# Order of the parts of y, quarter-array score products and the first weight signs in a fused gated-recurrence and SwiGLU kernel

## The chip, the cores and the metric

The kernel runs on one core of a Trainium2 chip. A core has five engines that work side by side: TensorE (PE) for matrix products, VectorE (DVE) and ScalarE (ACT) for elementwise work, GpSimd (POOL), and SyncE (SP), which only issues DMAs here. Products go to PSUM[...]; other operands lie in SBUF. The metric is the time of the whole program on the device, in microseconds, lower is better. A profile is one execution recorded instruction by instruction.

## The reference

Two stages in 32-bit floats. First a gated linear recurrence over 4 batches, 8 heads, 768 steps and head size 48:

```python
f = 1.0 / (1.0 + np.exp(-f_logit))
for t in range(S):
    state = f[:, :, t, :, None] * state + np.einsum('bhd,bhe->bhde', k[:, :, t], v[:, :, t])
    y[:, :, t] = np.einsum('bhd,bhde->bhe', q[:, :, t], state)
```

Its output is laid out as 3072 tokens of 384 numbers, and then a feed-forward block is computed with weights of 384x1536, 384x1536 and 1536x384:

```python
g = x @ w_gate
silu = g * (1.0 / (1.0 + np.exp(-g)))
val = x @ w_val
return silu * val @ w_out
```

The weights arrive as 64-bit floats and are turned into 32-bit ones on the chip.

## The kernel before, in words

**Tiling.** A unit is one chunk of 128 steps of one batch: six chunks c by four batches b, 24 units, in the order of chunks. Within a unit, two heads share the 128 partitions: one in rows 0 to 47, one in rows 64 to 111 (`par` is 0 or 1), and there are four such pairs (`a`). Running products of the gates scale k and q (`kT`, `qT`), so that a chunk needs no loop over steps. The function `attention(u)` is a generator with 15 steps per unit:

- *Scores* (L695 to L700): for each head, kT times qT, a 128x128 square, into two banks, one for each `par`. The contraction runs over 48 rows, so two heads can be in the array at once.
- *Mask* (L719): DVE multiplies the two banks with the causal triangle into `A`.
- *State decay* (L599): `decayed` is the state of the chunk before, times the chunk's whole decay.
- *y* (L734 to L759): for b = 0, 1, 2 and c > 0, y is built transposed in two banks from two parts. The state's part is `decayed` times `qT` (L742), with 48 rows and 64 columns, so it uses quadrants of the array. The masked part is v times `A` (L746), with 128 rows and 64 columns. ACT copies both banks to `yT` (L750), and ten small DMAs carry the heads to their rows of `xT[c]` (L757), through SP in chunk 1 and through POOL afterwards. For b = 3, and for chunk 0, another form is used (L767) that ACT copies straight into xT; its state part uses a block-diagonal copy of the state, `diagonal`.
- *dS* (L785 to L789): k transposed times v, the chunk's addition to the state, in column halves of the array. The last chunk has none. Then DVE (ACT in chunk 0) adds it to the state (L794, L797).

**Feed-forward.** Chunk 0 is computed plainly (`mlp_plain`, L836 and L859), beside the conversion of the weights. Chunks 1 to 5 use a scheme with 15 products in place of 18 for the hidden layer (L1052) and 7 in place of 8 for the output (L1151, L1214), with sums of weights and tokens made by DVE.

**Weights.** `weight_piece` makes a piece of 32-bit weights from 64-bit ones in two steps. `sizes` runs on ACT: a copy of the low words (L491), for pieces in the list `SIGNED` also a Sign operation on the top 16 bits (L494), and an absolute value (L495). `join` runs on DVE: a clamp (L505), a shift (L508, or L512 with a second operation), for pieces that are not in `SIGNED` a masking of the top 16 bits (L514), and an addition (L502, L510 or L516). The first two pieces are split in two parts each, of 128x384; the others have 128x768.

**Order.** PE, DVE, ACT and SP have a fixed order (`in_order`): steps of `attention` and of the weights are placed among the feed-forward products by written due times (`EARLY`, `JOINS_AT`, `SCORES`, `CHAINS`; `in_turn_of_time`). In chunks 2 to 5 the y of unit b, its dS and the scores of unit b+1 come due at the same moment (`times`: y at o, dS at o + 0.01, scores at s + 0.02, where o of one unit is s of the next), so on PE they stand one behind the other. In chunk 1 they are apart. Banks for scores come from a shared pool of attention banks, or from the pools of the feed-forward products (`score_bank`); from chunk 2 on the attention pool has three banks, used in turn.

Of the kernel before, what the change touches and what calls it, by code (L numbers as in the profile page):

```python
# [9 lines left out]
FP32 = mybir.dt.float32  # L10
# [280 lines left out]
def short_path(ctx, tc, ident, least, judge, q, k, v, f_logit, moe_w_gate, moe_w_val, moe_w_out, out):  # L291
# [9 lines left out]
    nc = tc.nc  # L301
    B, H, S, D = q.shape
    C = 128
    NCH = S // C
    HP = H // 2
    W = 64
# [9 lines left out]
    SQUARES = 2  # L316
# [3 lines left out]
    att = ctx.enter_context(tc.tile_pool(name="att", bufs=1))  # L320
# [30 lines left out]
    start = const.tile([128, HP * N1], FP32, tag="start", name="start")  # L351
# [27 lines left out]
    decayed = const.tile([128, HP, W], FP32, tag="decayed", name="decayed")  # L379
# [53 lines left out]
    def load(u, what="fkqv"):  # L433
        b, c = units[u]
        rows = slice(c * C, (c + 1) * C)
        inputs = dict(f=f_logit, k=k, q=q, v=v)
        for nm in "fqkv" if c >= SQUARES else "fvkq" if by_squares(u) else "fkqv":
            src = inputs[nm]
            if nm not in what:
                continue  # L440
            if nm == "v":
                dst = v_of(u)
            elif not by_squares(u):
                dst = raw[nm][u % NRAW]
            else:
                since = len(traced)
                for n in range(4):
                    at = Q * (1 - n % 2)
                    (nc.sync if c >= SQUARES else nc.gpsimd).dma_start(
                        out=rooms[nm][Q * n:Q * (n + 1), at:at + HP * RUN].rearrange("t (a e) -> t a e", a=HP),  # L450
                        in_=src[b, n // 2::2, rows, :].rearrange("a (t i) d -> t a (i d)", i=NI))
                if c < SQUARES:
                    by_pool.extend(ins for ins in traced[since:] if ins.engine == mybir.EngineType.Pool)
                    keep_order(by_pool[-5:])
                continue
            queue = nc.gpsimd if nm == "v" and c < SQUARES and (by_squares(u) or u in (1, 2)) else nc.sync
            queue.dma_start(out=dst[:, :, 0:D], in_=src[b, :, rows, :].rearrange("h t d -> t h d"))
# [71 lines left out]
    NW = 2  # L529
    FIRST = 2  # L530
    NPART = 2
    SIGNED = (4, 6, 7, 8, 9, 11, 15, 16, 17)

    def add_piece(dst, src, parts=1):
        fetch, *rest = weight_piece(dst, src, parts, len(fetches) in SIGNED)
        fetches.append(fetch)
        for group, fs in zip((sizes, joins), rest):
            group += fs
# [13 lines left out]
    xT = {}  # L552

    def rows_of(par):
        return slice(W * par, W * par + D)
# [3 lines left out]
    def bank(name):  # L559
        return banks[-1].tile([128, 512], FP32, tag="a", name=name)  # L560
# [15 lines left out]
    def attention(u):  # L576
        b, c = units[u]
# [58 lines left out]
        kT = att.tile([128, HP, C], FP32, tag="kT", name="kT")  # L636
        qT = att.tile([128, HP, C], FP32, tag="qT", name="qT", bufs=2)
# [8 lines left out]
        n = HP * N1  # L646
# [17 lines left out]
        if turned:  # L664
# [5 lines left out]
            for r in range(NI):  # L670
                turn_queue.dma_start(out=turn[:, :, :, r, :].rearrange("t i a e -> t (i a) e"),
                                  in_=beside[Q * r:Q * (r + 1)].rearrange("t i (a e) -> t (i a) e", e=Q))
# [23 lines left out]
        sc = [score_bank(u) for _ in range(2)]  # L696
        for a in range(HP):
            for par in range(2):
                r = rows_of(par)
                nc.tensor.matmul(sc[par][:, a * C:(a + 1) * C], lhsT=kT[r, a, :], rhs=qT[r, a, :], start=True, stop=True)  # L700
        if c < NCH - 1 and not turned:
            p = bank("kt")
            for a in range(HP):
# [26 lines left out]
        if c and b < B - 1:  # L730

            y = [bank("y") for _ in range(2)]  # L734

            def place(a, par):
                return y[par][W * (a % 2):W * (a % 2) + W, a // 2 * C:(a // 2 + 1) * C]

            for a in range(HP):
                for par in range(2):  # L740
                    r = rows_of(par)
                    nc.tensor.matmul(place(a, par), lhsT=decayed[r, a, :], rhs=qT[r, a, :],  # L742
                                     start=a < 2, stop=False, skip_group_check=True)
            for par in range(2):
                for a in range(HP):
                    nc.tensor.matmul(place(a, par), lhsT=v_[:, 2 * a + par, :], rhs=A[:, par, a, :],  # L746
                                     start=False, stop=a >= HP - 2, skip_group_check=True)
            yT = att.tile([128, 2, HP // 2 * C], FP32, tag="x", name="yT")
            for par in range(2):
                nc.scalar.copy(yT[:, par, :], y[par][:, 0:HP // 2 * C])  # L750
            for h in range(H):
                a, par = h // 2, h % 2
                f = h * D
                while f < (h + 1) * D:
                    n = min((h + 1) * D, (f // 128 + 1) * 128) - f
                    r = W * (a % 2) + f - h * D
                    (nc.gpsimd if c >= SQUARES else nc.sync).dma_start(out=xT[c][f % 128:f % 128 + n, f // 128, b * C:(b + 1) * C],  # L757
                                                                       in_=yT[r:r + n, par, a // 2 * C:(a // 2 + 1) * C])
                    f += n  # L759
        else:  # L760


            y = bank("y")
            met = set()

            def add(n, lhsT, rhs, last):
                nc.tensor.matmul(y[Q * (n % 4):Q * (n % 4) + Q, n // 4 * C:(n // 4 + 1) * C], lhsT=lhsT, rhs=rhs,  # L767
                                 start=n % 4 not in met, stop=last, skip_group_check=True)
                met.add(n % 4)

            per = 2 * D // Q
            if c:
                for n in range(DM // Q):
                    add(n, diagonal[:, n // per, n % per * Q:(n % per + 1) * Q], qT[:, n // per, :], False)
            flat = v_.rearrange("t h e -> t (h e)")
            for par in range(2):
                for n in range(DM // Q):
                    h = n // per * 2 + par
                    at = n * Q - h * D
                    if -Q < at < D:  # L780
                        add(n, flat[:, W * h + at:W * h + at + Q], A[:, par, h // 2, :], par == 1 or at + Q <= D)
            nc.scalar.copy(xT[c][:, :, b * C:(b + 1) * C], y[:, 0:DM].rearrange("p (a t) -> p a t", t=C))
        yield
        if c < NCH - 1:
            p = bank("dS")  # L785
            for h in range(H):
                nc.tensor.matmul(p[W * (h % 2):W * (h % 2) + W, (h // 2) * D:(h // 2 + 1) * D],  # L787
                                 lhsT=kt[:, h * W:(h + 1) * W], rhs=v_[:, h, 0:D], start=True, stop=True)
            dS = p[:, 0:HP * D].rearrange("p (a d) -> p a d", d=D)  # L789
        if c >= SQUARES and u + 2 < len(units):  # L790
            load(u + 2, "v")
        yield
# [134 lines left out]
    def score_bank(u):  # L927
        b, c = units[u]
        kind = SCORES[c][b][1] if c >= SQUARES else "b"
        if kind == "b":  # L930
            return bank("sc")
        return {"o": banks_o, "A": banks_a}[kind].tile([128, 512], FP32, tag=kind, name="sc")
# [316 lines left out]
    mark = traced[-1]  # L1249
    keep_warm(5)  # L1250
    first = [attention(b) for b in range(B)]
    done = [0] * B

# [47 lines left out]
    for b, at in enumerate(EARLY):  # L1301
        run_of = attention(B + b)
        waiting += [(t, lambda run_of=run_of: next(run_of)) for t in at]
# [22 lines left out]
    for c in range(2, NCH):  # L1326
        for b in range(B):
            run = attention(c * B + b)
            waiting += [((c - 2) * whole + t, lambda run=run: next(run)) for t in times(c)[b]]
# [21 lines left out]
def kernel(  # L1351
# [22 lines left out]
    def judge(bank):  # L1374
# [13 lines left out]
        yield  # L1388

    short_path(tc, ident, least, judge, *args)  # L1390
    with tc.If(redo[0] > 0, label="redo"):
        general_path(tc, *args)
# [32 lines left out]
```

## Time and profile before

| what | value |
|---|---|
| median of 3 runs | 597.59 us (597.56 to 597.68) |
| the profiled execution | 597.51 us, its span 595.8 us |
| PE busy | 585.5 us (98% of the span) |
| DVE busy | 479.3 us (80%) |
| ACT busy | 301.1 us (51%) |
| POOL busy | 112.8 us (19%) |
| granted TensorE clock | 1.000 |

The span is the time from the first to the last instruction of the profile; the rest of the execution lies around it. Busy is the time in which an engine has at least one instruction running. Matmuls overlap each other in the records, so the distance from one start to the next start tells more than the length of a record. Names such as L742 are lines of the kernel. In a row of a group, `out<-in` are tiles, then come the rows and columns of the array, the moving operand's size, the number of records, the busy time in us, the mean length in ns, and the engine's idle time ahead of them with what ended it.

### The profile page before, as it was taken

How to read it: one execution, taken by the hardware profiler on the slowest of the kernel's cores; microseconds unless marked ns; L12 is line 12 of the kernel's file. 1: busy time of each engine (PE TensorE's matmuls, PEld its weight loads, DVE VectorE, ACT ScalarE, POOL GpSimd, SP SyncE). 2: the span in 40 equal slices, each digit the busy share in tenths (PEclk: the TensorE clock that was granted, in tenths of full speed). 3: DMA queues.
4: the chain of work that ended last, by engine and by line, in shares of the span. 5: the costliest groups of instructions: out<-in, count | busy, mean ns of one | idle time of the engine just before them, and what ended most of it. 6: DMA issues, size and time to landing. Idle time of an engine off the chain costs nothing.

```text
span 595.8 us, 10874 instructions
## 1 busy us (share of the span) xinstructions
PE 585.5 (98%) x3972; PEld 481.8 (81%) x3972; DVE 479.3 (80%) x830; ACT 301.1 (51%) x563; POOL 112.8 (19%) x240
## 2 busy tenths in 40 slices
PE   7899999999999999999999999999999999999996
PEld 4744444667888999888999888899988899988896
DVE  7997998999989877998986888994978972666741
ACT  3488677025877322676640667632476730356600
POOL 3140345202132330212030030330030330000000
PEclk9999999999999999999999999999999999999999
DMA  9999487233666565542345332543231100100001
GB/s 205 253 307 286 142 217 186 60 98 107 122 117 110 96 150 136 138 100 64 84 117 137 99 80 62 112 111 99 74 99 28 29 10 6 53 2 1 2 1 56
DMA packets 106291, 61.86 MB, mean 104 GB/s; under 512 B 64200, under 2 KB 97032, under 8 KB 106232
## 3 DMA queue, kind: packets, MB, share of 16 engines
q1 hardware_dynamic: 93800, 45.96, 31.0%
q0 software_dynamic: 10992, 13.19, 10.0%
q10 hardware_dynamic: 1440, 1.97, 0.9%
q8 instruction: 32, 0.52, 0.4%
q14 instruction: 27, 0.22, 0.1%
HBM read 47.64 MB, written 8.13 MB: 94 GB/s over the span
## 4 chain that ended last, share of the span: by engine, by line
PE 98%; DVE 1%; ACT 0%; issue 0%; DVEq 0%
PE o L1151 20%; PE A L1052 18%; PE B L1052 15%; PE c L1052 6%; PE o L1052 6%; PE o L859 5%; PE gate L836 5%; PE val L836 5%; PE sc L700 4%; PE o L1214 3%; PE y L746 3%; PE y L767 2%; PE dS L787 2%; PE y L742 2%; PE kt L704 1%; PE fTp L614 0%
## 5 line engine op out<-in xcount | busy, mean ns | idle before, releaser
L757 POOL DMA_DIRECT2D xT<-yT x120 | 59.8, 506 | 53.4 <-ACT yT L750 49.0
L1052 PE MATMUL A<-xs,w_both 128*128 128x256 f32 x240 | 62.2, 382 | 0.0
L1151 PE MATMUL o<-w_out,h 128*128 128x192 f32 x360 | 62.0, 327 | 0.0
L1151 PEld LDWEIGHTS o<-w_out,h 128*128 128x128 f32 x360 | 58.7, 190 | 1.0 <-issue 0.2
L1057 ACT COPY c<-A 128x512 f32<-128x512 f32 x40 | 23.3, 583 | 60.5 <-PE A L1052 59.4
L1057 ACT COPY aside<-A 128x512 f32<-128x512 f32 x60 | 35.2, 586 | 32.9 <-PE A L1052 32.7
L951 DVE TENSOR_TENSOR c<-c,aside 128x512 f32<-128x512 f32 x60 | 41.1, 685 | 12.8 <-ACT aside L1057 11.1
L1052 PEld LDWEIGHTS A<-xs,w_both 128*128 128x128 f32 x240 | 44.9, 190 | 6.6
L1004 DVE TENSOR_TENSOR h<-h,c 128x256 f32<-128x256 f32 x100 | 40.6, 414 | 7.6 <-ACT h L1068 7.3
L954 DVE TENSOR_TENSOR c<-c,aside 128x512 f32<-128x512 f32 x60 | 41.0, 684 | 2.7 <-ACT aside L1057 2.7
L1068 ACT ACTIVATE h<-c 128x256 f32<-128x256 f32 x100 | 39.4, 417 | 5.0 <-DVE c L951 3.8
L719 DVE TENSOR_TENSOR A<-sc,causal 128x512 f32<-128x512 f32 x48 | 30.9, 685 | 13.4 <-PE sc L700 13.4
L1151 PE MATMUL o<-ws,h 128*128 128x192 f32 x240 | 41.5, 328 | 0.0
L1052 PE MATMUL B<-xs,w_both 128*128 128x256 f32 x160 | 41.3, 380 | 0.0
L1052 PE MATMUL A<-xs,extra 128*128 128x256 f32 x160 | 41.2, 380 | 0.0
L1052 PE MATMUL c<-xT,w_both 128*128 128x256 f32 x160 | 41.1, 379 | 0.0
L1052 PE MATMUL B<-xT,extra 128*128 128x256 f32 x160 | 41.0, 379 | 0.0
L1057 ACT COPY aside<-B 128x512 f32<-128x512 f32 x60 | 35.2, 586 | 9.0 <-PE B L1052 7.0
L1151 PEld LDWEIGHTS o<-ws,h 128*128 128x128 f32 x240 | 39.1, 190 | 0.5
L954 DVE TENSOR_TENSOR c<-o,c 128x512 f32<-128x512 f32 x40 | 27.4, 686 | 11.0 <-ACT h L1068 6.2
L951 DVE TENSOR_TENSOR c<-c,o 128x384 f32<-128x384 f32 x15 | 8.2, 548 | 34.8 <-PE o L1151 34.8
L690 POOL MEMSET gates<- 128x4 f32 x24 | 3.6, 150 | 169.0 <-DVE qT L593 163.9
(163 smaller groups left out, 1240.2 us busy)
## 6 DMA issues: line engine op xcount, KB each, us to landing
fsquares<-in_f_logit_dram SPq DMA_DIRECT2D x64, 96.0 KB, 4.1
qsquares<-in_q_dram SPq DMA_DIRECT2D x64, 96.0 KB, 2.3
ksquares<-in_k_dram SPq DMA_DIRECT2D x64, 96.0 KB, 2.4
w<-in_moe_w_gate_dram SPq DMA_DIRECT2D x6, 768.0 KB
w<-in_moe_w_val_dram SPq DMA_DIRECT2D x6, 768.0 KB, 6.5
w<-in_moe_w_out_dram SPq DMA_DIRECT2D x6, 768.0 KB, 8.8
v<-in_v_dram SPq DMA_DIRECT2D x19, 192.0 KB, 2.8
turn<-ksquares SPq DMA_DIRECT2D x40, 64.0 KB, 2.2
```

What stands on the lines that cost most here:

```text
L700: nc.tensor.matmul(sc[par][:, a * C:(a + 1) * C], lhsT=kT[r, a, :], rhs=qT[r, a, :], start=True, stop=True)
L719: nc.vector.tensor_tensor(A[:, par], sc[par].rearrange("p (a t) -> p a t", t=C), causal.unsqueeze(1).broadcast_to((128, HP, C)), ALU.mult)
L757: (nc.gpsimd if c >= SQUARES else nc.sync).dma_start(out=xT[c][f % 128:f % 128 + n, f // 128, b * C:(b + 1) * C], in_=yT[r:r + n, par, a / ...
L836: nc.tensor.matmul(p, lhsT=w[:, j, i, :], rhs=xT[c][:, i, :], start=(i == 0), stop=(i == KT - 1))
L859: nc.tensor.matmul(p, lhsT=hidden_tile(h, n // 2)[:, n % 2 * 2 + b // 2, b % 2 * C:(b % 2 + 1) * C], rhs=w_out[:, j, :], start=(n == 0), s ...
L951: nc.vector.tensor_tensor(dst, a, b, ALU.add)
L954: nc.vector.tensor_tensor(dst, a, b, ALU.subtract)
L1004: lagging.append(lambda: f(*args))
L1052: nc.tensor.matmul(p[name][:, n, :], lhsT=weights_of[a][:, n, j, :], rhs=tokens[b], start=fresh and n == 0, stop=True, skip_group_check=True)
L1057: nc.scalar.copy(t, p[name])
L1068: nc.scalar.activation(dst, src[:, 0, :], AF.Silu)
L1151: nc.tensor.matmul(p[:, n, :], lhsT=lhsTs[j][:, n * C:(n + 1) * C], rhs=rhs[:, j, :], start=first and j == order[0] and n == 0, stop=j == ...
```

## The change

Three edits. First, for c > 0 and b < 3 the masked part of y is now computed first and opens the accumulation, dS follows, and the state's part is added after dS, with the copies and DMAs of y behind it (`add_state`). For the last chunk there is no dS and the state's part comes directly after the masked part, one step later in the generator. Second, for c > 0 each score product is split in two column halves, so that it uses a quadrant of the array. Third, pieces 0 and 1 of the weights join the list `SIGNED`.

```diff
-    SIGNED = (4, 6, 7, 8, 9, 11, 15, 16, 17)
+    SIGNED = (0, 1, 4, 6, 7, 8, 9, 11, 15, 16, 17)
...
-                nc.tensor.matmul(sc[par][:, a * C:(a + 1) * C], lhsT=kT[r, a, :], rhs=qT[r, a, :], start=True, stop=True)
+                for half in range(2) if c else ():
+                    nc.tensor.matmul(sc[par][W * half:W * half + W, a * C:(a + 1) * C], lhsT=kT[r, a, W * half:W * half + W],
+                                     rhs=qT[r, a, :], start=True, stop=True)
+                if c == 0:
+                    nc.tensor.matmul(sc[par][:, a * C:(a + 1) * C], lhsT=kT[r, a, :], rhs=qT[r, a, :], start=True, stop=True)
...
-            for a in range(HP):
-                for par in range(2):
-                    r = rows_of(par)
-                    nc.tensor.matmul(place(a, par), lhsT=decayed[r, a, :], rhs=qT[r, a, :],
-                                     start=a < 2, stop=False, skip_group_check=True)
             for par in range(2):
                 for a in range(HP):
                     nc.tensor.matmul(place(a, par), lhsT=v_[:, 2 * a + par, :], rhs=A[:, par, a, :],
-                                     start=False, stop=a >= HP - 2, skip_group_check=True)
...
+                                     start=a < 2, stop=False, skip_group_check=True)
+
+            def add_state():
+                for a in range(HP):
+                    for par in range(2):
+                        r = rows_of(par)
+                        nc.tensor.matmul(place(a, par), lhsT=decayed[r, a, :], rhs=qT[r, a, :],
+                                         start=False, stop=a >= HP - 2, skip_group_check=True)
...
             dS = p[:, 0:HP * D].rearrange("p (a d) -> p a d", d=D)
+        if c and b < B - 1:
+            add_state()
```

The copies to `yT` and the ten DMAs, left out above, move into `add_state` unchanged.

More of the change, by code (lines that the diff above doesn't have):

```diff
@@ L746, in attention @@
                     nc.tensor.matmul(place(a, par), lhsT=v_[:, 2 * a + par, :], rhs=A[:, par, a, :],
-                                     start=False, stop=a >= HP - 2, skip_group_check=True)
[L748 to L759, printed above, removed]
+                                     start=a < 2, stop=False, skip_group_check=True)
[5 more added lines that the diff above has]
+                                         start=False, stop=a >= HP - 2, skip_group_check=True)
+                yT = att.tile([128, 2, HP // 2 * C], FP32, tag="x", name="yT")
+                for par in range(2):
+                    nc.scalar.copy(yT[:, par, :], y[par][:, 0:HP // 2 * C])
+                for h in range(H):
+                    a, par = h // 2, h % 2
+                    f = h * D
+                    while f < (h + 1) * D:
+                        n = min((h + 1) * D, (f // 128 + 1) * 128) - f
+                        r = W * (a % 2) + f - h * D
+                        (nc.gpsimd if c >= SQUARES else nc.sync).dma_start(out=xT[c][f % 128:f % 128 + n, f // 128, b * C:(b + 1) * C],
+                                                                           in_=yT[r:r + n, par, a // 2 * C:(a // 2 + 1) * C])
+                        f += n
         else:
```

## The prediction

> **What bounds the kernel now.** I read the page's first part and its chain, then the groups by shape, the order in time around one change of unit, and last, wait by wait, how long before each TensorE instruction its operands were ready.
>
> ```profile
> PE 585.5 (98%) x3972; PEld 481.8 (81%) x3972; DVE 479.3 (80%) x830; ACT 301.1 (51%) x563; POOL 112.8 (19%) x240
> ...
> PE 98%; DVE 1%; ACT 0%; issue 0%; DVEq 0%
> ```
>
> TensorE is the path from 29.6 us to the end, so what it saves is worth its full time unless another engine's result comes too late. The groups that change, by shape:
>
> ```profile
> L700 PE MATMUL sc<-qT,kT 48*128 48x128 f32 x384 | 27.9, 284 | 2.5 <-DVE qT L593 1.6 <-ACT least L712 0.5 <-ACT state L794 0.4
> ...
> L746 PE MATMUL y<-A,v 128*64 128x128 f32 x240 | 16.4, 279 | 0.0
> L787 PE MATMUL dS<-v,kt 128*64 128x48 f32 x320 | 12.9, 223 | 0.0
> L742 PE MATMUL y<-qT,decayed 48*64 48x128 f32 x240 | 10.0, 282 | 0.0
> ```
>
> Each matmul leaves two records (x240 is 120 matmuls, 8 per unit). Scores use two row halves, the state's part four quadrants, the masked part and dS two column halves, everything large the whole array. One unit, in order of time on PE (start, length):
>
> ```profile
> 166.13 0.59 PE L1052 MATMUL A<-xT,w_both 128*128 128x256 f32 x2
> 166.66 0.67 PE L742 MATMUL y<-qT,decayed 48*64 48x128 f32 x16
> 167.25 1.09 PE L746 MATMUL y<-A,v 128*64 128x128 f32 x16
> 168.18 0.62 PE L787 MATMUL dS<-v,kt 128*64 128x48 f32 x16
> 168.73 1.16 PE L700 MATMUL sc<-qT,kT 48*128 48x128 f32 x16
> 169.82 0.66 PE L704 MATMUL kt<-idf,kT 128*128 128x128 f32 x4
> ```
>
> Start to start: state part 0.60, masked part 0.92, dS 0.55, scores 1.09, together 3.165. At chunk 5, where no dS follows, the masked part takes longer:
>
> ```profile
> 434.73 1.09 PE L746 MATMUL y<-A,v 128*64 128x128 f32 x16
> 435.75 1.16 PE L700 MATMUL sc<-qT,kT 48*128 48x128 f32 x16
> ```
>
> 1.02 against 0.92: between masked part and dS (one cut of the array) there is no gap, and before another cut there is one of 0.10. The single records say the same. In the state part groups of four start 0.109 apart (the first interval 0.160), in the scores groups of two 0.112 apart (the first 0.214). So a new cut costs 0.10 of emptying and an extra first load of 0.05 (64 columns) or 0.10 (128 columns). The state part is 4 x 0.109 + 0.05 + 0.11 = 0.60, the scores 8 x 0.112 + 0.10 + 0.10 = 1.09.
>
> **The skill.** The Trainium skill, "TensorEngine Tiling (Array Packing)", section "Tiling Modes", says that changing the tiling mode, not just the tile, drains TensorE, and that different tiles load and multiply in parallel: the 0.10 and the groups of four agree. Its section "Restrictions and Gotchas" says different row tiles must not use one PSUM bank at once; the new scores keep one bank per row half, as the state part does. "TensorE: Matmul & The Clock Gate", section "LDWEIGHTS (loading the stationary operand)", says the load goes by columns: 0.188 us records at 128 and 0.133 at 64 have the same direction.
>
> **The change, part by part.**
>
> 1. Scores in quadrants (20 units, chunks 1 to 5): twice the matmuls at half the columns. Price from the state part: eight groups of four at 0.109. That pace holds for long: 24 and 32 records of the quarter-column form take 0.68 and 1.01 at 224.82. Alone, a score block is 0.87 + 0.05 + 0.105 = 1.03 against 1.093: 0.065 less. Eight blocks stand alone (four of chunk 1, b=0 of chunks 2 to 5): 0.52.
>
> 2. The new order. In the built program the twelve other blocks (chunks 2 to 5, b=1 to 3) directly follow the state part, now of the same cut. The wait for qT that stands between them in PE's queue does not stall it where qT is there in time (0.7 to 4 us ahead in eleven of the twelve). Before, state and scores took 0.597 + 1.093 = 1.690. After: twelve groups at 0.109, one first load 0.05, one emptying 0.105: 1.464. Masked part and dS keep 0.925 and 0.55 (at chunk 5, 1.02). Saved 0.226 a block, 2.71 in twelve. In chunk 1 the state part moves behind dS with whole-array work after it: as many cuts, 0.
>
> 3. The y copies (L750) wait for the last state matmul: the first is ready some 0.8 later, the second 0.45, and with them the DMAs on POOL (SP in chunk 1; b=1 there moves past four gate products, 88.6 to about 95.6). The unit's ten DMAs follow on POOL (5.06 us from 168.85), with the gates memset behind them, which a scan needs only several us later; xT is read when the next chunk's products begin, 20 us and more after b=2. In chunk 1 they are on SP: b=1's ten, 89.0 to 99.2, move to about 96 to 106 behind the v load that now passes them, and the next writer of that yT room comes at 110.6. Behind the copies ACT idles 2.55 at 168.8; at 249.5 and 278.6 a sigmoid ends as late as the new y. PE's nearest reader is the kt transpose at 169.82, which takes the first y bank: ready 1.25 early before, about 0.35 now. Next is the diagonal copy of chunk 1, used 2.9 after it ends. Both hidden; without cover up to 0.5.
>
> 4. Signs of the first two pieces: four fewer masking operations on DVE (0.59 each, L514), four more Signs on ACT. No 128x384 Sign is in the trace; the 128x768 one is 1.15, the 128x384 copy of the same tile 0.65 against 1.08, so about 0.65 (0.5 to 0.7). The first L514 delays a mask that PE waits for:
>
> ```profile
> 26.13 0.59 DVE L514 TENSOR_SCALAR up<-w 128x384 uint16<-128x384 uint16 x1
> 26.35 0.66 PE L704 MATMUL kt<-idf,kT 128*128 128x128 f32 x4
> 26.60 1.28 DVE L719 TENSOR_TENSOR A<-sc,causal 128x512 f32<-128x512 f32 x2
> ```
>
> Other units start this mask 1.16 after the scores' start; here that would be 26.41. Gain 0.19. Cost: ACT runs some 0.95 later at 37.6, DVE's next join waits for it, and qT of the next scores (46.04, ready 1.26 early) is left with about 0.1. Taken as 0, up to 0.2.
>
> Two DVE times eat part of this. First, c=2, b=3:
>
> ```profile
> 211.00 0.69 DVE L593 TENSOR_TENSOR qT<-tails,gates 128x512 f32<-128x512 f32 x1
> ...
> 211.83 1.16 PE L700 MATMUL sc<-qT,kT 48*128 48x128 f32 x16
> ```
>
> These scores already wait 0.07 for qT. Its chain runs unbroken from the copy of `o` at 200.58 (ACT), which waits for PE at 200.5; no PE saving after that pulls it in. The blocks at 202.55 and 211.83 thus cannot save 0.45; only what the latter saves after its start counts, about 0.09. Lost: 0.36.
>
> Second, the planner now puts one sum into xT ahead of DVE's second ob copy:
>
> ```profile
> 139.41 0.55 DVE L880 COPY ob<-o 128x384 f32<-128x384 f32 x1
> 139.87 0.75 DVE L951 TENSOR_TENSOR xT<-xT 128x256 f32<-128x256 f32 x2
> 140.17 1.03 PE L1052 MATMUL o<-xT,w_both 128*128 128x256 f32 x4
> ```
>
> The product at 140.17 takes the bank that this copy empties (done 139.97). The sum is 0.38, so done 140.35, product at 140.4; it would otherwise come at 140.1, as DVE here last waited for PE at 114.24 and PE saves only one block, 0.065, since. Lost: 0.28.
>
> Sum: 2.71 + 0.52 + 0.19 - 0.36 - 0.28 = 2.78. The profiled execution took 597.51 (span 595.8, 1.7 around it), 0.08 under the median: span 593.0, median 597.59 - 2.78 = **594.8 us**.
>
> **Rivals.** (a) The array still empties between state part and scores, because the scores' own wait or new row tiles break the stream. Then each of 20 blocks saves only 0.065: 1.30 + 0.19 - 0.28 = 1.2, 596.4. For: no place before has this pair. Against: masked part into dS, two different operand pairs, runs through. (b) New waits: the kt transpose, the chunk-1 scores and the copies cost 0.5 to 2 more, 595.3 to 596.8. For: margins of 0.1 and 0.35. Against: most PE waits on DVE have 0.7 or more. (c) Slower: score matmuls that sit side by side in one row half do not overlap, since unlike the state part (which alternates row halves) consecutive ones share moving data and bank. Groups then take 0.218: 160 groups x 0.109 = 17.4 more, 612.2. It decides from a pace of 0.126 (2.78 / 160 above 0.109). Against: the column halves of L746 overlap at 0.109 a pair. (d) Little is lost to DVE: 0.6 better, 594.2.
>
> **How the numbers follow.** Forecast with (d) as its better edge 0.70, (a) 0.12, (b) 0.13, (c) 0.05. A measurement tells 0.2%, 1.2 us: faster below 596.4, slower above 598.8. (a) lies on the border, half to each; of (b) a quarter is above: faster 0.86, same 0.09, slower 0.05. Range 593.8 (both DVE losses absent, ends of the estimates) to 596.2 (most of (b)). It leaves out (a), (c) and the worst quarter of (b): 0.2.
>
> **What would show it.** PE, start to start: scores alone 1.03, state part to the end of the scores 1.46, no gap between them; the mask at 26.4 and the gate product at 29.4; the `o` product near 140 right behind the ob copy; scores of c=2, b=3 right behind qT. A group pace above 0.12, a gap of 0.1 ahead of the scores, or a wait at the kt transposes would make it wrong.

## The result and the profile after

The changed kernel takes 595.06 us (median of 6 runs, 595.0 to 595.35), beside 597.93 us for the kernel before (median of 6 runs): a ratio of 0.9952, 95% interval 0.9942 to 0.9962. In a second comparison it was 595.04 against 597.56, ratio 0.996 (0.9946 to 0.9973). The profiled execution took 595.19 us with a span of 593.5 us, against 597.51 and 595.8 before: 2.3 us less. The forecast was 2.8 us less. In the two comparisons the medians differ by 2.9 and 2.5 us, and both intervals hold the forecast's ratio of 0.9953.

The first and fourth part of the page, of the kernel after:

```profile
PE 583.6 (98%) x4292; PEld 480.6 (81%) x4292; DVE 477.1 (80%) x826; ACT 303.2 (51%) x567; POOL 112.2 (19%) x240
...
PE 96%; DVE 2%; ACT 0%; issue 0%; DMA 0%; ACTq 0%; DVEq 0%
```

TensorE has 320 more records (two for each of 160 added score matmuls) and is still the path. DVE's share in the chain rises from 1% to 2%: the chain now runs mostly through VectorE from 203.7 to 211.4 us, ahead of the scores of chunk 2, b=3, which wait for it. Below, the cut of a part is the way in which it divides the array: whole, in row or column halves, or in quadrants. The unit shown before, in order of time on PE (start, length):

```profile
166.57 1.10 PE L745 MATMUL y<-A,v 128*64 128x128 f32 x16
167.49 0.62 PE L794 MATMUL dS<-v,kt 128*64 128x48 f32 x16
168.04 0.67 PE L752 MATMUL y<-qT,decayed 48*64 48x128 f32 x16
168.53 1.05 PE L701 MATMUL sc<-qT,kT 48*64 48x128 f32 x32
169.52 0.66 PE L708 MATMUL kt<-idf,kT 128*128 128x128 f32 x4
```

Masked part and dS still take 0.92 and 0.55 from start to start. State part and scores take 1.47 (1.471 in the single records) where they took 1.690. The last record of the state's part starts 0.089 ahead of the scores' first, the spacing of two groups within a part (0.199 in the old order, where another cut followed): the gap of a change of cut is gone. The scores' groups of four run at 0.109.

The same places in the two traces follow. The lead is the time by which an instruction on PE starts earlier than the same one in the kernel before; a step is what the lead gained since the row above.

| place (time before, us) | lead, us | step, us | forecast step, us |
|---|---|---|---|
| first gate product, 29.6 | 0.152 | 0.152 | 0.19 |
| after the four score blocks of chunk 1, 120.4 | 0.380 | 0.228 | 0.26 |
| second record of the `o` product, 140.4 | 0.032 | -0.348 | -0.28 |
| chunk 2, b=0 and 1: 170.3 | 0.305 | 0.273 | 0.29 |
| chunk 2, b=2 and 3: 212.9 | 0.363 | 0.058 | 0.09 |
| scores of b=0, chunks 3 to 5 | | 0.175 | 0.195 |
| nine other blocks, chunks 3 to 5; 487.8 | 2.494 | 1.956 | 2.03 |
| end of the span | 2.33 | -0.17 | 0 |

The last row belongs to the last output's DMA: the span ends 4.56 after DVE's last sum, 4.39 before. A second profile of the same kernel had 4.37 and a span of 593.3, so this is scatter.

The wait near 140 us, first on DVE, then on PE, of the kernel after:

```profile
139.08 0.41 DVE L960 TENSOR_TENSOR xT<-xT 128x256 f32<-128x256 f32 x1
139.41 0.55 DVE L889 COPY ob<-o 128x384 f32<-128x384 f32 x1
```

```profile
138.93 1.03 PE L1061 MATMUL B<-xs,w_both 128*128 128x256 f32 x4
140.06 0.89 PE L1061 MATMUL o<-xT,w_both 128*128 128x256 f32 x3
```

The product comes 1.13 behind its neighbour (0.86 before), as the copy that empties its bank ends at 139.96. Its second record is late by another 0.075 (0.291 behind the first, where 0.216 is the pace): the load of its weights starts 0.077 behind the first record, while in the kernel before it starts with it.

### The profile page after: what moved, and what is told of

Its sections match the earlier page's. It is cut to its first block, busy times and chain, and to the rows that moved or that the text cites. A ratio compares the mean times of both kernels' runs of the same rounds, so it can differ in the third digit from the quotient of the medians.

```text
span 593.5 us, 11514 instructions
## 1 busy us (share of the span) xinstructions
PE 583.6 (98%) x4292; PEld 480.6 (81%) x4292; DVE 477.1 (80%) x826; ACT 303.2 (51%) x567; POOL 112.2 (19%) x240
## 4 chain that ended last, share of the span: by engine, by line
PE 96%; DVE 2%; ACT 0%; issue 0%; DMA 0%; ACTq 0%; DVEq 0%
PE o L1160 19%; PE A L1061 18%; PE B L1061 15%; PE o L1061 6%; PE c L1061 6%; PE o L868 5%; PE gate L845 5%; PE val L845 5%; PE o L1223 3%; PE sc L701 3%; PE y L745 2%; PE y L774 2%; PE dS L794 2%; PE y L752 1%; PE sc L704 1%; PE kt L708 1%
## 5 line engine op out<-in xcount | busy, mean ns | idle before, releaser
L723 DVE TENSOR_TENSOR A<-sc,causal 128x512 f32<-128x512 f32 x48 | 30.8, 681 | 11.9 <-PE sc L701 11.6
L1061 PEld LDWEIGHTS B<-xs,w_both 128*128 128x128 f32 x160 | 30.2, 190 | 4.6 <-ACT c L1066 0.4
```

Of the source, the lines that this page charges most:

```text
L723: nc.vector.tensor_tensor(A[:, par], sc[par].rearrange("p (a t) -> p a t", t=C), causal.unsqueeze(1).broadcast_to((128, HP, C)), ALU.mult)
L1061: nc.tensor.matmul(p[name][:, n, :], lhsT=weights_of[a][:, n, j, :], rhs=tokens[b], start=fresh and n == 0, stop=True, skip_group_check=True)
```

## The experiments

The theory: time is saved where two neighbouring parts have the same cut of the array, so that a change of cut falls away; a little comes from the shorter first load of the quadrants; the rest of the change moves waits. The rivals: the order itself saves; the quadrants themselves save; the two waits on VectorE belong to something else. All leads below are from single records of the traces.

### The order alone

The changed kernel with the score loop and the list of signs of the kernel before.

```diff
...
-                for half in range(2) if c else ():
-                    nc.tensor.matmul(sc[par][W * half:W * half + W, a * C:(a + 1) * C], lhsT=kT[r, a, W * half:W * half + W],
-                                     rhs=qT[r, a, :], start=True, stop=True)
-                if c == 0:
...
+                nc.tensor.matmul(sc[par][:, a * C:(a + 1) * C], lhsT=kT[r, a, :], rhs=qT[r, a, :], start=True, stop=True)
```

> The new order alone: masked part, dS, state's part; scores in two row halves as before, the first two pieces' signs on VectorE as before. My theory (what is saved is a change of the array's cut between state's part and scores, and it exists only if both have the same cut): state's part (quadrants) into scores (row halves) is still a change, so masked part 0.925, dS 0.55, state 0.60, scores 1.09 add up to 3.165 as before, and the time is the one of before within 0.3 us (ratio 0.9995 to 1.0005). Rival (the order itself saves, because dS and the masked part go first): 0.2 us in each of twelve places, 2 us or more in all, ratio about 0.996.

Measured: 597.55 us against 597.55, ratio 1.0004 (0.9997 to 1.0011). The unit in order of time on PE:

```profile
166.51 1.09 PE L741 MATMUL y<-A,v 128*64 128x128 f32 x16
167.43 0.62 PE L790 MATMUL dS<-v,kt 128*64 128x48 f32 x16
167.98 0.67 PE L748 MATMUL y<-qT,decayed 48*64 48x128 f32 x16
168.58 1.16 PE L700 MATMUL sc<-qT,kT 48*128 48x128 f32 x16
169.67 0.66 PE L704 MATMUL kt<-idf,kT 128*128 128x128 f32 x4
```

0.92, 0.55, 0.60 and 1.09: the four numbers of the kernel before, in another order. In this trace PE leads the kernel before by 0.14 to 0.15 from its first scores (9.74 against 9.88) to the end, apart from the parts that change places; a lead that is there before the first changed instruction is not the change's. The rival falls.

### The quadrants alone

The kernel before with the new score loop.

> Scores in quadrants alone, in the old order, signs as before. My theory: every one of the 20 score blocks stands alone, 1.035 from start to start in place of 1.093, 1.15 us saved in 20; 0.06 of it is lost at the scores of chunk 2, b=3, which wait for qT, and 0.35 at the product near 140 us, since this build too has one token sum ahead of the copy that empties the product's bank. Span about 595.05, 0.7 us shorter, ratio about 0.9988. Rival (quadrants save most of it by themselves): 2 us or more, ratio 0.9965 or less.

Measured: 596.81 us, ratio 0.9986 (0.998 to 0.9993). The unit in order of time on PE, from dS on:

```profile
168.24 0.62 PE L791 MATMUL dS<-v,kt 128*64 128x48 f32 x16
168.79 1.10 PE L701 MATMUL sc<-qT,kT 48*64 48x128 f32 x32
169.82 0.66 PE L708 MATMUL kt<-idf,kT 128*128 128x128 f32 x4
```

Each score block is 0.057 shorter, PE leads by 0.709 after the last scores, and 0.355 was lost at 140 us, in this build too. The forecast of 0.7 holds, and the rival falls. So the parts give 0 and 0.7 on PE, and both together, without the signs, 2.4 (the run without the signs, below): most of the saving is made by the pair. It also shows that the score loop alone brings the planner's exchange of sum and copy; the order alone doesn't have it.

### One part moved, two cuts more

The changed kernel, with `add_state()` called directly after the masked part.

```diff
...
+            add_state()
         else:
...
-        if c and b < B - 1:
-            add_state()
```

> The changed kernel with one thing moved: the state's part directly behind the masked part and ahead of dS. The same instructions, two more changes of the cut in nine places (chunks 2 to 4) and one more in two units of chunk 1; none more in chunk 5. My theory: masked 1.02, state 0.60, dS 0.60, scores 1.035 in place of 0.925, 0.55, 0.487, 0.984: 0.31 more in nine places, 0.15 in two, less 0.4 that is waited for qT anyway in chunk 2: 2.4 to 2.8 us slower than the changed kernel, span about 596.1, ratio to before about 1.000. Rival (it is the pace of the quadrant scores and the earlier dS that gain, not the cuts): at most 0.3 us slower than the changed kernel, ratio about 0.9955.

Measured: 597.77 us, ratio 1.0003 (0.9994 to 1.0011), 2.64 us behind the changed kernel on PE after the last scores.

```profile
166.86 1.09 PE L745 MATMUL y<-A,v 128*64 128x128 f32 x16
167.88 0.67 PE L752 MATMUL y<-qT,decayed 48*64 48x128 f32 x16
168.48 0.67 PE L795 MATMUL dS<-v,kt 128*64 128x48 f32 x16
169.08 1.10 PE L701 MATMUL sc<-qT,kT 48*64 48x128 f32 x32
170.12 0.66 PE L708 MATMUL kt<-idf,kT 128*128 128x128 f32 x4
```

Every instruction of the changed kernel is here, masked part first and quadrant scores included, and the gain is gone. The unit takes 3.26 in place of 2.95. The steps in the lead are 0.312 in each of eight places, 0.151 in each of two units of chunk 1, and in the ninth place 0.137 is won back, since these scores no longer reach their wait for qT early (0.45 of waiting, with the slower start behind it, falls away against 0.312). A change of cut thus costs 0.15 to 0.16, half of 0.312: 0.10 of gap and 0.05 for a first load of 64 columns. This is the run that shows the cause: its time and that of the changed kernel have intervals that do not meet. The traces show the 0.10 as time, not what the array does in it.

### The signs

The changed kernel without pieces 0 and 1 in the list.

```diff
-    SIGNED = (0, 1, 4, 6, 7, 8, 9, 11, 15, 16, 17)
+    SIGNED = (4, 6, 7, 8, 9, 11, 15, 16, 17)
```

> The changed kernel with the first two pieces' signs back on VectorE. My theory: the mask of chunk 0, b=3 starts at 26.6 again and the first gate product at 29.62, 0.15 us later than in the changed kernel, and nothing else differs: span about 593.6, ratio about 0.9955. Rival (ScalarE's added work costs more later than the mask gains): faster than the changed kernel, first gate product at 29.62 but scores of chunk 1, b=0 not later than 45.9.

Measured: 595.29 us, ratio 0.9963 (0.9949 to 0.9977). On DVE:

```profile
26.12 0.59 DVE L514 TENSOR_SCALAR up<-w 128x384 uint16<-128x384 uint16 x1
26.59 1.27 DVE L723 TENSOR_TENSOR A<-sc,causal 128x512 f32<-128x512 f32 x2
```

In the changed kernel no L514 stands there:

```profile
26.44 1.29 DVE L723 TENSOR_TENSOR A<-sc,causal 128x512 f32<-128x512 f32 x2 [0.23 <-PE sc L704]
```

Without the signs the mask starts at 26.59 again, the first gate product at 29.60, 0.132 behind the changed kernel, and 0.116 of this distance is left at the end. The signs are worth 0.12 to 0.15 us. On a time this can't be told: the intervals of the two kernels overlap.

### The two waits on VectorE

First, an order edge puts the token sum behind the copy again; `emptied` holds the copies of the plain outputs.

```diff
             plus(b12, b11, b12)
+            if c == 1:
+                tc.add_manual_dep(traced[-1], emptied[-1][0].name, mybir.DependencyInfo(
+                    mybir.DependencyClass.NoSync, mybir.DependencyReason.DATA), reason="order")
             plus(b31, b11, b31)
```

> The changed kernel with an order edge that puts the token sum into xT behind VectorE's second copy of the plain outputs, as the planner had it before. My theory: the o product near 140 us no longer waits, 0.35 us gained (0.27 of waiting and 0.08 of a first load behind it), span about 593.1. Rival (the wait there belongs to something else, such as ScalarE's copy or the DMAs of xT): no change, the product stays 0.49 behind its neighbour.

Measured: 594.76 us, ratio 0.9951 (0.9936 to 0.9967). The product follows its neighbour by 0.87 again (138.92 and 139.79), PE gains 0.273 and then 0.060 at its second record, and the gain stays. The wait is the copy's. In the time this cannot be told from the changed kernel, as the intervals overlap; the same holds for the next run.

Second, the sigmoid of chunk 2, b=3, with which the chain to the waiting scores begins, comes due a step earlier. In the changed kernel these scores wait for qT behind the state's part:

```profile
210.64 0.67 PE L752 MATMUL y<-qT,decayed 48*64 48x128 f32 x16
211.53 1.10 PE L701 MATMUL sc<-qT,kT 48*64 48x128 f32 x32 [0.22 <-DVE qT L593]
```

```diff
...
+        if c == 2:
+            sigmoid[3] = down[1] - 0.02
```

> The changed kernel with the sigmoid of chunk 2, b=3 due one step of the output products earlier, so that it goes ahead of ScalarE's copy of o at 200.3. My theory: the chain of VectorE that ends in qT of these scores starts about 0.55 us earlier, the scores at 211.5 no longer wait (0.40 waited, 0.05 of a first load), span about 593.05, 0.38 to 0.45 us shorter. Rival (VectorE's own backlog of h sums holds the chain, not ScalarE): qT no earlier than 0.1 us, no change.

Measured: 594.57 us, ratio 0.9948 (0.9933 to 0.9963). ACT of this run, in order of time:

```profile
198.11 1.28 ACT L619 ACT_TABLE_LOAD   x1
199.41 0.63 ACT L619 ACTIVATE fsquares<-fsquares 128x512 f32<-128x512 f32 x1
200.35 0.48 ACT L1181 COPY c<-o 128x384 f32<-128x384 f32 x1 [0.32 <-PE o L1162]
```

In the changed kernel the same load and sigmoid stood behind the copy, at 200.78 and 202.07. DVE's transpose now starts at 202.19, right behind its own sums, qT is done at 210.96 instead of 211.38, and on PE the state's part and the scores are neighbours again:

```profile
210.71 0.67 PE L752 MATMUL y<-qT,decayed 48*64 48x128 f32 x16
211.20 1.05 PE L701 MATMUL sc<-qT,kT 48*64 48x128 f32 x32
```

0.49 in place of 0.89. The step in the lead is 0.449: 0.40 of waiting and 0.05 of a first load. ScalarE's place in the chain was what mattered, as the theory had it; VectorE's backlog takes over only 0.6 us earlier.

### Both, and the scores of chunk 0

Both edits together, and the same with the new score loop in chunk 0 as well.

```diff
-                for half in range(2) if c else ():
+                for half in range(2):
...
-                if c == 0:
...
```

> The edits of the two runs before together. My theory: they are independent and add up, 0.7 to 0.8 us shorter than the changed kernel, span about 592.7, ratio to before about 0.994.

> The same, and the scores of chunk 0 in quadrants as well. My theory: only the last of these four blocks is what the next mask waits for, so the first gate product comes 0.06 us earlier, at 29.41, and the span is 592.6. Rival (each of the four lies on the path): 0.23 us earlier.

Measured: both 594.21 us, ratio 0.9944 (0.993 to 0.9957), PE 0.80 ahead of the changed kernel from 212.6 on; the two gains add up. With chunk 0: 594.82 us, with single times from 594.03 to 595.99, ratio 0.9959 (0.9946 to 0.9973); on PE the first gate product came 0.16 earlier than with both, not 0.06 (the scores of b=1, 2, 3 start at 15.04, 20.14, 25.14 in place of 15.07, 20.20, 25.24). It looked as if part of each block's saving gets through. But these starts also shift without an edit: in the run with the early sigmoid, whose chunk 0 is that of the changed kernel, the scores of b=2 and 3 start 0.05 and 0.08 later than in that kernel. The three kernels were then measured side by side.

> The changed kernel itself, beside the two below on one chip, so that the three can be compared. TensorE ahead of the kernel before by 2.49 us once the last scores are done, give or take 0.15 of the start; 2.3 to 2.9 us shorter in time, ratio 0.995 to 0.996.

> Both waits on VectorE taken away: 0.7 to 0.8 us shorter than the changed kernel in the same call. If the two waits were only shifted to the end, it would be within 0.2 us of it.

> The scores of chunk 0 in quadrants too: TensorE 0.16 us ahead of the run before this from the first gate product on, as once seen, and 0.1 to 0.2 us shorter in time. If that lead was only the scatter of the start, 0 within 0.1.

Measured on one chip, against 597.56 for the kernel before: the changed kernel 595.04 (0.996, 0.9946 to 0.9973), both 594.22 (0.9948, 0.9935 to 0.9962), chunk 0 as well 594.25 (0.9955, 0.9941 to 0.9969). PE's lead after the last scores was 2.50, 3.27 and 3.35. Both edits give 0.8 us over the changed kernel, as expected, and are the best version found: nine of their ten runs took 594.16 to 594.38 us, and none of the changed kernel's eleven was below 595.0. With chunk 0 as well, the lead over both edits was 0.08 this time, 0.16 the other, and the time shows nothing of it. So the expected repeat of 0.16 and of 0.1 to 0.2 us in the time did not come, and whether chunk 0 gains stays open.

## Why the prediction was right

The forecast of 594.8 us lies 0.2 to 0.3 from the measured 595.0. This is not luck of errors that cancel: in the table every step up to the last scores falls a little short of its forecast, 0.28 in sum. Point by point:

- *Price of a change of cut.* Right. It was read from two rows that differ only in what follows the masked part; the run with the state's part moved shows it alone, 0.312 for two.
- *Twelve adjacent blocks, 0.226 each.* Right, a little high: 0.218. A state part and scores in one stream take 1.471, not 1.464.
- *Eight blocks alone, 0.065 each.* Right, 0.057: 1.035 in place of the 1.03 that was summed up.
- *Signs, 0.19.* Right in its mechanism, 0.15 in size: the mask started at 26.44, not 26.41. The cost was close: the 128x384 Sign takes 0.72, just outside the 0.5 to 0.7 that was given, ACT was 0.95 late at 37.7 as forecast, and the scores of chunk 1, b=0 had 0.17 left where 0.1 was forecast.
- *Scores of chunk 2, b=3.* Right: they started at the same distance from the release of the chain as before, and both blocks together gave 0.06 (forecast 0.09).
- *The product near 140.* Right in place and cause; 0.28 forecast, 0.35 measured. The wait itself was 0.273; what was left out is its end, the second record that is late by 0.075. Extra first loads of that kind had been read off the changes of cut (0.05 to 0.10) and were not used here.
- *What was costed at nothing.* The kt transpose had its bank 0.38 early (0.35 forecast), and no PE wait came from the later y copies or their DMAs. The margins of qT in eleven of the twelve blocks are wider than the 0.7 to 4 us that were read: 0.96 to 11.9 in the profile before, 0.86 to 11.9 after. This only helps the argument.
- *Rivals.* (a) falls by the 0.089 between state part and scores, (c) by the pace of 0.109; (b) by the two margins above. Of (d) nothing came by itself; the runs without the two waits are this case, and gave 594.2, its number.

## What to carry to other kernels

When matmuls of several array cuts stand side by side, put those of one cut next to each other, and where operands allow it recut one of them so that they match: ahead of what went into waits, the order alone was worth 0, the recut alone 1.1 us, and both together 3.1. Price such a change by the distance from start to start of neighbouring parts, since record lengths overlap. Then look, for each place where the bound engine gains, how long before its start its operands were ready: 0.8 us of this gain went to two waits, one with a margin of 0.2 us before and one with none, and one order edge and one earlier due time brought it back.

## What the runs showed that had not been expected

The first scores of an execution started at 9.74 us in one profile and at 9.87 or 9.88 in the others, and the output's last DMA ended 4.34 to 4.69 us after the last sum: up to 0.14 us at the start and 0.35 us at the end of a single span is scatter. Comparing leads at the same instruction, place by place, showed steps of 0.06 us that the times could not show. And the wait for a bank near 140 us cost more than the wait: 0.06 to 0.08 us more, at the second record behind it.
